# A filter MLP layer by four 64-row tiles, its decay factor moved into the weights, and a transform that begins with the filter

## The chip, the cores and the metric

The kernel runs on one core of a Trainium2 chip. Its time is the device time of one execution in microseconds (us), taken over several runs. TensorE (PE) multiplies matrices, VectorE (DVE), ScalarE (ACT) and GpSimd (POOL) work element by element, and SyncE (SP) issues most of the DMA transfers. PEld is the part of TensorE that loads the stationary operand of a matmul.

## The reference

```
h_mlp  = relu(pos_emb @ w1) @ w2          # 12480 x 64, 64 x 64, 64 x 128
h_filt = h_mlp * exp(-0.01 * pos)         # the window, pos = 0 .. 12479
u      = x * v                            # 12480 x 128
y      = causal convolution of u with h_filt along the sequence, by FFT
a      = x * y
g1 = a @ w_in;  b = (g1 * clip(g1 + 3, 0, 6) / 6) @ w_out        # 128 -> 2048 -> 128
g2 = b @ w_in2; out = elu(g2) @ w_out2                           # 128 -> 2048 -> 128
```

In float32 the window is exactly zero from position 10398 on, so only the first 10398 rows of the filter matter.

## The kernel before, in words

The sequence is folded into 98 blocks of 128 positions (`H1 = 98`, `N2 = 128`); inside a block, position 64+i and position 63-i are paired, for i from 0 to 63 (`HN = 64`). So each i is a column of 98 pairs. The convolution is a transform over the block index (the *first step*, line 324), one over the position inside a block (lines 378, 387, 397), a product (411, 416), and the way back (424, 504). Two MLPs of 2048 hidden units follow (lines 624 to 668), and take most of the time. All engines follow one order written out by hand; nothing reorders it. An engine that waits holds up whatever stands behind it.

The change is at the very start:

- SP loads the position embeddings in eight pieces (line 169, tile `qb<-in_posT`; the pieces end at i = 4, 10, 17, 25, 34, 44, 54, 64), then six chunks of x and v (`uv<-in_xc`, `uv<-in_vc`), and between these the small tables `ratio`, `t1`, `rows`, `column`. Eight transfers are in flight: the ninth is issued when the first has landed, and so on.
- `filter_hidden` (lines 274 to 306) works on groups of columns: i = 0..3, 4..7, then eight at a time, then 56..59 and 60..63. One matmul per i (line 278) has the 98 pairs as its stationary operand, with the 64 features of one position in the upper 64 rows and those of its partner in the lower 64, and a block-diagonal `w1` of 128 columns as the moving one. `relu` (line 286) is done by ACT for the second half, i by i, with the decay ratio of the two partners as its scale. `folds` (line 299) has DVE take the relu of the first half and add and subtract the second; the sums and differences are the *filter pieces'* input `Rf`.
- `signal` (lines 262 to 271) multiplies a chunk of x and v (4 channels) and makes sums and differences. Chunks 0 and 1 are done by POOL, the others by DVE.
- The first step has 48 units of eight matmuls (`first`, line 320): 32 take a signal chunk (`first_u`, kind 0 in `order`), 16 take 4 features of the filter (`first_r`, kind 1). Each ends in one ACT copy (line 327). `first_r` reads all 64 columns of `Rf`, so no such unit can begin before the last fold.

Of the kernel before, what the change touches and what calls it, by code (L numbers as in the profile page):

```python
# [41 lines left out]
NU = KF // 2  # L42
LAG, DELAY = 5, 13
EX = 8
HIDDEN = [(0, 4), (4, 4), *((i, 8) for i in range(8, HN - 8, 8)), (HN - 8, 4), (HN - 4, 4)]
WARM = 6
LEAST, MOST = (float(np.uint32(z).view(np.float32)) for z in (0x38000000, 0x47EFFFFF))

# [11 lines left out]
def tables():  # L60
    n1, k1, k2 = np.arange(H1), np.arange(NK), np.arange(N2)
    i, m, a = np.arange(HN), np.arange(NM), np.arange(H1) - 2 * SHIFT - 1
    w = 2 * np.pi * (np.outer(n1 - SHIFT, k1) % N1) / N1
    c, s = np.cos(w), np.sin(w)

    t1 = np.stack([np.stack([c, -s], axis=2), np.stack([-s, -c], axis=2)], axis=1)
    k = k1[:, None] + N1 * k2
    w = np.pi * (((2 * i + 1)[:, None, None] * k) % (2 * L)) / L
    gm = np.concatenate([np.cos(w), np.sin(w)], axis=0)

    w = 2 * np.pi * (np.outer(k2, m) % N2) / N2
# [12 lines left out]
    rows = t1 * np.exp(-0.01 * N2 * n1)[:, None, None, None]
    column = np.tile(np.exp(-0.01 * (HN + i)), 2)[:, None]
    ratio = np.tile(np.repeat(RATIO, 2), (H1, 1))
    return [np.ascontiguousarray(z, dtype=np.float32) for z in (t1, gm, cs, ti, rows, column, ratio)]


def folded(z):  # L90

    z = np.pad(z, ((0, SP - S), (0, 0))).reshape(H1, N2, -1)
    return np.stack([z[:, HN:], z[:, HN - 1::-1]], axis=1).transpose(0, 3, 1, 2)


@with_exitstack
def tile_kernel(ctx, tc, xc, vc, xT, posT, w1_d, w2_d, moe_w, t1_d, gm_d, cs_d, ti_d, rows_d, column_d, ratio_d, outT):
    nc = tc.nc
    w_dram = [nc.dram_tensor(f"w_scratch{i}", (128, FF), F32, kind="Internal").ap() for i in range(4)]

# [34 lines left out]
    qb = big.tile([128, 2 * QW], F32, name="qb")  # L135
# [22 lines left out]
    assert MB + MW <= RF and RF + D + MW <= 2 * QW - AW - RW  # L158

    pos_t = qb[:, :HP]  # L160
    Rf = qb[:H1, RW:RW + RF].rearrange("p (g s i t) -> p s i g t", s=2, i=HN, t=2)
    Rp = qb[:H1, RW:RW + RF].rearrange("p (g s x) -> p s g x", s=2, x=2 * HN)
    w1s = qb[:, HP:HP + 2 * FO]
    ratio = qb[:H1, HP + 2 * FO:HP + 2 * FO + N2]
    GI = 4
    nc.scalar.dma_start(w1s, w1_d)
    edges = [0, 4, 10, 17, 25, 34, 44, 54, 64]
    for a, b in zip(edges, edges[1:]):
        nc.sync.dma_start(pos_t[:, a * H1:b * H1], posT[:, a * H1:b * H1])
    tab = const.tile([128, 8 * NK], F32, name="tab")  # L170
    t1, rows = (tab[:H1, i * 4 * NK:(i + 1) * 4 * NK].rearrange("p (f k) -> p f k", f=2) for i in range(2))
    qss = [z[:NK, :4 * N2].rearrange("p (d n) -> p d n", n=N2) for z in (tab, au[:, AW:], au[:, S:])]
    thirds = [0]
    column = const.tile([128, 1], F32, name="column")
    cs = const.tile([128, 2 * N2], F32, name="cs")
# [77 lines left out]
    NR = FO // DC  # L253
# [17 lines left out]
        return ut  # L271


    def filter_hidden(i0, n):
        pr = bank("pr", [128, 2, 2, FO // 2, GI, 2])
        t = au[:H1, i0 * FO:(i0 + n) * FO].rearrange("p (b g j t) -> p b g j t", g=FO // 2, j=GI, t=2)
        for j in range(n):
            nc.tensor.matmul(  # L278
                pr[:H1, j // GI, :, :, j % GI], lhsT=pos_t[:, (i0 + j) * H1:(i0 + j + 1) * H1],
                rhs=w1s.rearrange("p (s g t) -> p s g t", s=2, t=2), start=True, stop=True,  # L280
            )
        def relu(b):
            i = i0 + b * GI
            own = GI if i < HN - 2 * GI else 2
            for j in range(own):
                nc.scalar.activation(t[:, b, :, j], pr[:H1, b, 1, :, j], AF.Relu, scale=float(RATIO[i + j]))
            return own

        def folds(b, own):
            i = i0 + b * GI  # L290
            if own < GI:
                nc.vector.scalar_tensor_tensor(
                    t[:, b, :, own:].rearrange("p g j t -> p g (j t)"),
                    pr[:H1, b, 1, :, own:].rearrange("p g j t -> p g (j t)"), 0.0,
                    ratio[:, 2 * (i + own):2 * (i + GI)].unsqueeze(1).to_broadcast([H1, FO // 2, 2 * (GI - own)]),
                    op0=ALU.max, op1=ALU.mult,
                )
            for x, op in enumerate((ALU.add, ALU.subtract)):
                nc.vector.scalar_tensor_tensor(
                    Rp[:, x, :, 2 * i:2 * (i + GI)], pr[:H1, b, 0].rearrange("p g j t -> p g (j t)"), 0.0,  # L300
                    t[:, b].rearrange("p g j t -> p g (j t)"), op0=ALU.max, op1=op,
                )

        owns = [relu(b) for b in range(n // GI)]
        for b, own in enumerate(owns):
            folds(b, own)

    for n in range(DEEP):
        load_signal(n)
        if n == 0:  # L310
            nc.sync.dma_start(ratio, ratio_d)
            nc.sync.dma_start(t1.rearrange("p f k -> p (f k)"), t1_d)
        if n == 1:
            nc.sync.dma_start(rows.rearrange("p f k -> p (f k)"), rows_d)
            nc.sync.dma_start(column, column_d)
# [222 lines left out]
    for m0 in range(0, NM, 2):  # L538
# [208 lines left out]
```

## Time and profile before

| | |
|---|---|
| three runs | 1347.17, 1348.6, 1349.86 us; median 1348.6 |
| profiled execution | span 1346.2 us, from the first to the last instruction; no other time is shown for it |
| busy | PE 99%, PEld 85%, DVE 85%, ACT 74%, POOL 29% of the span |
| filter MLP and its folds | 3.8 to 22 us |
| first step of the transform | 19.4 to 79.1 us |

The share of busy time is an average over the whole program, in which the two MLPs weigh most. The change touches the first 80 us, so it is read from the timeline and the chain of waits there. The timeline prints runs of equal instructions as one row: where it starts, how long it lasts, engine, line, operation, tiles, count, and in brackets the idle time ahead of it with what ended it. One matmul of 32-bit numbers leaves two PE records and two PEld records. In the trace, a row named SPq or ACTq is the issue of a DMA.

### The profile page before, as it was taken

What the parts mean: (1) busy time and instruction counts of PE and PEld (TensorE: products, weight loads), DVE (VectorE), ACT (ScalarE), POOL (GpSimd) and SP (SyncE); (2) the same over time, 40 slices, a digit from 0 to 9 for tenths busy, and PEclk for the clock granted to TensorE, in tenths of its full rate; (3) what the DMA queues carried; (4) which work ended last, traced back from release to release, by engine and by line L of the source; (5) the groups of instructions that cost most, each with busy time, mean ns of one, the idle gap of its engine ahead of it and who ended that gap; (6) DMA issues with size and microseconds to landing.
All of it is one profiled execution on the core that took longest, in us unless ns stands there. A gap on an engine that the chain in (4) does not pass through costs nothing.

```text
span 1346.2 us, 20841 instructions
## 1 busy us (share of the span) xinstructions
PE 1338.7 (99%) x8154; PEld 1148.0 (85%) x8154; DVE 1149.3 (85%) x1230; ACT 992.9 (74%) x1171; POOL 394.4 (29%) x280
## 2 busy tenths in 40 slices
PE   9999999999999999999999999999999999999998
PEld 9999999978888888888888888888888888888898
DVE  6749887799988888888888888888888888888897
ACT  5666633288788877788778878887778877887876
POOL 1027721215322222332222232222233222222223
PEclk9999999999999999999999999999999999999999
DMA  8924319730000000000000000000000000000000
GB/s 268 258 75 142 100 34 293 237 106 1 8 0 9 8 9 9 1 8 9 9 0 9 9 9 1 8 9 9 9 1 8 9 9 1 9 8 9 9 3 17
DMA packets 32490, 58.15 MB, mean 43 GB/s; under 512 B 3879, under 2 KB 12168, under 8 KB 32392
## 3 DMA queue, kind: packets, MB, share of 16 engines
q1 hardware_dynamic: 25192, 48.11, 11.7%
q10 hardware_dynamic: 7200, 8.72, 2.0%
q8 instruction: 64, 1.05, 0.3%
q14 instruction: 34, 0.28, 0.1%
HBM read 46.23 MB, written 10.58 MB: 42 GB/s over the span
## 4 chain that ended last, share of the span: by engine, by line
PE 90%; DVE 5%; issue 2%; ACT 1%; POOL 1%; DMA 1%; SPq 0%; POOLq 0%; DVEq 0%; ACTq 0%
PE h L624 37%; PE o L668 37%; PE pa L324 4%; PE q L424 4%; PE y L504 3%; PE z L397 1%; DVE gs L658 1%; PE pr L278 1%; DVE bp L411 1%; DVE qb L411 1%; PE r L378 1%; PE h L387 1%; DVE cv L210 1%; DVE g L645 1%; DMA qb<-in_posT 0%
## 5 line engine op out<-in xcount | busy, mean ns | idle before, releaser
L668 PE MATMUL o<-gs,w 128*128 128x512 f32 (+1 forms) x2400 | 567.1, 384 | 0.5 <-DVE gs L658 0.3
L668 PEld LDWEIGHTS o<-gs,w 128*128 128x128 f32 x2400 | 445.3, 188 | 88.6 <-DVE gs L658 0.8
L637 POOL TENSOR_SCALAR a<-a 128x1024 f32<-128x1024 f32 (+1 forms) x200 | 294.5, 1472 | 720.0 <-ACT a L636 720.0
L658 DVE TENSOR_TENSOR gs<-g,gs 128x1024 fp32r<-128x1024 f32 (+1 forms) x400 | 482.4, 1206 | 4.5 <-ACT gs L653 3.7
L653 ACT CAST gs<-g 128x1024 fp32r<-128x1024 f32 (+1 forms) x400 | 410.2, 1025 | 54.4 <-DVE g L645 52.8
L645 DVE SCALAR_TENSOR_TENSOR g<-a,h 128x1024 f32<-128x1024 f32 (+1 forms) x200 | 238.6, 1193 | 121.4 <-ACT a L634 121.3
L624 PE MATMUL h<-xs,w 128*128 128x512 f32 (+1 forms) x1200 | 302.1, 387 | 0.4 <-DVE g L645 0.4
L624 PE MATMUL h<-x,w 128*128 128x512 f32 (+1 forms) x1200 | 299.0, 385 | 0.2 <-ACT a L636 0.2
L636 ACT ACTIVATE a<-h 128x1024 f32<-128x1024 f32 (+1 forms) x200 | 201.3, 1006 | 92.7 <-PE h L624 91.5
L624 PEld LDWEIGHTS h<-xs,w 128*128 128x128 f32 x1200 | 223.6, 188 | 48.5 <-DVE g L645 1.4
L624 PEld LDWEIGHTS h<-x,w 128*128 128x128 f32 x1200 | 223.0, 188 | 43.8 <-issue 0.5
L634 ACT ACTIVATE a<-h,bounds 128x1024 f32<-128x1024 f32 (+1 forms) x200 | 218.9, 1095 | 51.8 <-PE h L624 51.6
L647 DVE SCALAR_TENSOR_TENSOR g<-a,h 128x1024 f32<-128x1024 f32 (+1 forms) x200 | 237.2, 1186 | 0.2 <-POOL a L637 0.2
L215 POOL TENSOR_TENSOR cv<-cv 128x256 int32<-128x256 int32 x32 | 23.3, 729 | 96.4 <-DVE cv L212 89.8
L416 POOL TENSOR_TENSOR qb<-qb,bp 128x1024 f32<-128x1024 f32 (+2 forms) x14 | 27.7, 1981 | 71.2 <-DMA qb<-in_gm 70.7
L504 PE MATMUL y<-ti,qb 91*64 91x98 f32 (+1 forms) x1024 | 45.9, 247 | 0.8 <-DVE cv L212 0.5
L504 PEld LDWEIGHTS y<-ti,qb 91*64 91x64 f32 x1024 | 45.4, 138 | 1.3 <-DVE cv L212 0.7
L324 PE MATMUL pa<-tab,cv 98*64 98x182 f32 x512 | 44.5, 318 | 0.0
L324 PEld LDWEIGHTS pa<-tab,cv 98*64 98x64 f32 x512 | 37.6, 137 | 3.9
L198 ACT ACTIVATE cv<-cv 128x256 f32<-128x256 f32 x32 | 14.3, 447 | 35.1 <-DMA cv<-in_mw 16.8
L411 DVE TENSOR_TENSOR qb<-z,qb 128x1024 f32<-128x1024 f32 (+2 forms) x15 | 15.9, 1060 | 17.9 <-ACT qb L390 15.2
L431 DVE TENSOR_TENSOR qb<-q,au 91x512 f32<-91x512 f32 (+2 forms) x44 | 26.4, 650 | 3.8 <-ACT au L429 3.8
(67 smaller groups left out, 832.5 us busy)
## 6 DMA issues: line engine op xcount, KB each, us to landing
uv<-in_xc SPq DMA_DIRECT2D x32, 196.0 KB
out_T<-y SPq DMA_DIRECT2D x23, 256.0 KB
au<-in_xT SPq DMA_DIRECT2D x8, 728.0 KB
qb<-in_gm SPq DMA_DIRECT2D x22, 256.0 KB
ti<-in_ti SPq DMA_DIRECT2D x32, 139.3 KB
cv<-in_mw ACTq DMA_DIRECT2D x17, 256.0 KB
uv<-in_vc SPq DMA_DIRECT2D x22, 196.0 KB
w_scratch<-cv ACTq DMA_DIRECT2D x32, 128.0 KB
```

What stands on the lines that cost most here:

```text
L324: nc.tensor.matmul(pa[f * HN:(f + 1) * HN, j, :2 * NK], lhsT=src(j, f), rhs=table[:, f], start=True, stop=True)
L424: nc.tensor.matmul(q[:NK, r, j], lhsT=Au[hf][:, s0 + j, :, r], rhs=cs[:, r * N2:(r + 1) * N2], start=True, stop=True)
L504: nc.tensor.matmul(y[h * HD:(h + 1) * HD, off:off + w], lhsT=Q[:NK, h, j // 2, :, j % 2], rhs=ti[:, m - m0, r, H1 - w:], start=r == 0, sto ...
L624: nc.tensor.matmul(h[:, j], lhsT=wslice(2 * m - 2, a, 2 * u + j), rhs=x[:, b], start=i == 0, stop=i == 2)
L634: nc.scalar.activation(a, h, AF.Relu, bias=three)
L636: nc.scalar.activation(a, h, AF.Exp)
L637: nc.gpsimd.tensor_scalar(a, a, 1.0, 0.0, op0=ALU.min, op1=ALU.max)
L645: nc.vector.scalar_tensor_tensor(g, a, 6.0, h, op0=ALU.min, op1=ALU.mult)
L647: nc.vector.scalar_tensor_tensor(g, a, -1.0, h, op0=ALU.add, op1=ALU.max)
L653: nc.scalar.copy(t[:, 0], g)
L658: nc.vector.tensor_tensor(out=t[:, 1], in0=g, in1=t[:, 0].bitcast(F32), op=ALU.subtract)
L668: nc.tensor.matmul(o[:, :WID[t]], lhsT=wslice(2 * m - 1, a, 2 * u + j), rhs=gs[:, b, j], start=u == 0 and j == 0 and i == 0, stop=u == NU ...
```

## The change

The second half's decay ratio leaves the activation. It is multiplied into 64 copies of `w1`, one for each i (`w1x`), in partitions 64 to 127: the builds for the first five groups are done by DVE, those for the last four by POOL. Each i is then four matmuls of 64 rows, 64 output partitions and 64 columns: first and second half (r) times two overlapping sets of 64 of the 82 blocks that are left (a: blocks 0 to 63 and 18 to 81; in the table `rows`, the duplicated blocks have zeros). The positions are loaded for 82 blocks instead of 98, in the same eight pieces. `Rf` and the table `rows` now take 128 partitions, the relu and the folds work on 128 partitions and on all columns of a group in one instruction, and the last two groups of four become one of eight. For the groups at i = 24 and i = 48 (`SIDE`), ACT does the relu of both halves and POOL the sum and the difference. The table `ratio` and its load are gone. The first step begins with two filter units instead of two signal units.

```diff
+HR = -(-ZERO // N2)                       # 82
-HP = H1 * HN
+HP = HR * HN
+ROWS = np.concatenate([np.arange(HD), np.arange(HR - HD, HR)])
-HIDDEN = [(0, 4), (4, 4), *((i, 8) for i in range(8, HN - 8, 8)), (HN - 8, 4), (HN - 4, 4)]
+HIDDEN = [(0, 4), (4, 4), *((i, 8) for i in range(8, HN, 8))]
+SIDE = (24, 48)
...
-    w1s = qb[:, HP:HP + 2 * FO]
-    ratio = qb[:H1, HP + 2 * FO:HP + 2 * FO + N2]
+    w1s, ratio = qb[:, HP:HP + FO], qb[HD:, HP + FO:HP + FO + HN]
+    w1x = qb[HD:, HP + FO + HN:HP + FO + HN + HN * FO].rearrange("p (i g) -> p i g", g=FO)
+    nc.scalar.dma_start(qb[:, HP:HP + FO + HN], w1_d)
-        nc.sync.dma_start(pos_t[:, a * H1:b * H1], posT[:, a * H1:b * H1])
+        nc.sync.dma_start(pos_t[:, a * HR:b * HR], posT[:, a * HR:b * HR])
...
+    for k, (i0, n) in enumerate(HIDDEN):
+        (nc.vector if k < 5 else nc.gpsimd).tensor_tensor(
+            out=w1x[:, i0:i0 + n], in0=w1s[HD:].unsqueeze(1).to_broadcast([HD, n, FO]),
+            in1=ratio[:, i0:i0 + n].unsqueeze(2).to_broadcast([HD, n, FO]), op=ALU.mult,
+        )
...
         for j in range(n):
-            nc.tensor.matmul(
-                pr[:H1, j // GI, :, :, j % GI], lhsT=pos_t[:, (i0 + j) * H1:(i0 + j + 1) * H1],
-                rhs=w1s.rearrange("p (s g t) -> p s g t", s=2, t=2), start=True, stop=True,
-            )
+            for a in (0, 1):
+                for r, w in enumerate((w1s[:HD], w1x[:, i0 + j])):
+                    c = (i0 + j) * HR + a * (HR - HD)
+                    nc.tensor.matmul(
+                        pr[a * HD:(a + 1) * HD, r, :, j], lhsT=qb[r * FO:(r + 1) * FO, c:c + HD],
+                        rhs=w.rearrange("p (g t) -> p g t", t=2), start=True, stop=True,
+                    )
+        nc.scalar.activation(t, pr[:, 1, :, :n], AF.Relu)
+        if i0 in SIDE:
+            nc.scalar.activation(t0, pr[:, 0, :, :n], AF.Relu)
+        for x, op in enumerate((ALU.add, ALU.subtract)):
+            to = Rp[:, x, :, 2 * i0:2 * (i0 + n)]
+            a, b = (z.rearrange("p g j t -> p g (j t)") for z in ((t0 if i0 in SIDE else pr[:, 0, :, :n]), t))
+            if i0 in SIDE:
+                nc.gpsimd.tensor_tensor(out=to, in0=a, in1=b, op=op)
+            else:
+                nc.vector.scalar_tensor_tensor(to, a, 0.0, b, op0=ALU.max, op1=op)
...
-    order = [(0, n) for n in range(2)] + [(1, 0), (1, 1)]
-    for c in range(2, NR + 1):
-        order += [(0, 2 * c - 2), (0, 2 * c - 1)] + [(1, c)] * (c < NR)
+    order = [(1, 0), (1, 1)]
+    for c in range(2, NR + 2):
+        order += [(0, 2 * c - 4), (0, 2 * c - 3)] + [(1, c)] * (c < NR)
```

On PE, from the warm-up matmuls to the fifth unit of the first step (`pr` is the filter MLP, `pa` the first step; `cv` holds a signal chunk, `qb` the filter), it stood before:

```order
L131 MATMUL warm<-au 128x128 x6
L278 MATMUL pr<-qb 98x64x2 x64
L324 MATMUL pa<-tab,cv 64x182 x16
L324 MATMUL pa<-tab,qb 64x182 x16
L324 MATMUL pa<-tab,cv 64x182 x16
```

and now:

```order
L134 MATMUL warm<-au 128x128 x6
L293 MATMUL pr<-qb 64x32x2 x256
L323 MATMUL pa<-tab,qb 64x182 x16
L323 MATMUL pa<-tab,cv 64x182 x16
L323 MATMUL pa<-tab,qb 64x182 x8
```

Four small matmuls stand for each one of before, and the two signal units (16 matmuls) have changed places with the two filter units. On POOL, from its first tile operation to its last before the second step (`uv`, `cv` are signal chunks), it stood before:

```order
L267 TENSOR_TENSOR uv<-uv 98x512
L269 TENSOR_TENSOR cv<-uv 98x4x64
L270 TENSOR_TENSOR cv<-uv 98x4x64
L267 TENSOR_TENSOR uv<-uv 98x512
L269 TENSOR_TENSOR cv<-uv 98x4x64
L270 TENSOR_TENSOR cv<-uv 98x4x64
```

and now:

```order
L279 TENSOR_TENSOR qb<-qb 64x512 x4
L304 TENSOR_TENSOR qb<-au 128x32x16 x4
L271 TENSOR_TENSOR uv<-uv 98x512
L273 TENSOR_TENSOR cv<-uv 98x4x64
L274 TENSOR_TENSOR cv<-uv 98x4x64
L271 TENSOR_TENSOR uv<-uv 98x512
L273 TENSOR_TENSOR cv<-uv 98x4x64
L274 TENSOR_TENSOR cv<-uv 98x4x64
```

The two signal chunks that POOL prepares stand behind four builds of scaled weights and behind the folds of two groups. On DVE, from its first operation on the filter to the first signal chunk, it stood before:

```order
L299 SCALAR_TENSOR_TENSOR qb<-pr,au 98x32x8 x28
L292 SCALAR_TENSOR_TENSOR au<-pr,qb 98x32x4
L299 SCALAR_TENSOR_TENSOR qb<-pr,au 98x32x8 x2
L292 SCALAR_TENSOR_TENSOR au<-pr,qb 98x32x4
L299 SCALAR_TENSOR_TENSOR qb<-pr,au 98x32x8 x2
L267 TENSOR_TENSOR uv<-uv 98x512
```

and now:

```order
L279 TENSOR_TENSOR qb<-qb 64x256 x2
L279 TENSOR_TENSOR qb<-qb 64x512 x3
L306 SCALAR_TENSOR_TENSOR qb<-pr,au 128x32x8 x4
L306 SCALAR_TENSOR_TENSOR qb<-pr,au 128x32x16 x10
L271 TENSOR_TENSOR uv<-uv 98x512
```

Five builds of scaled weights stand ahead of the folds, and 32 folds of four columns have become 4 of four and 10 of eight.

## Rows read from the trace of the kernel before

**Rows 1.** Chain that ended last, 0 to 80 us: start us, us, what
```profile
1.65 5.66 DMA qb<-in_posT
...
7.36 12.03 PE pr L278 x108
19.39 59.74 PE pa L324 x728
79.13 3.77 PE r L378 x32
```
**Rows 2.** Groups of instructions by line, 4.5 to 5 us, then 6 to 6.5 us
```profile
L278 PE MATMUL pr<-qb 128*98 128x128 f32 x5 | 1.3, 421 | 0.0
...
L278 PE MATMUL pr<-qb 128*98 128x128 f32 x7 | 0.9, 273 | 0.0
```
**Rows 3.** Timeline of PE in later steps: start us, us, engine, line, operation, count
```profile
24.55 0.32 PE L324 MATMUL pa<-tab,cv 98*64 98x182 f32 x1
24.55 0.32 PE L324 MATMUL pa<-tab,qb 98*64 98x182 f32 x1
...
88.67 2.10 PE L387 MATMUL h<-qb 64*128 64x128 f32 x32
91.09 2.10 PE L397 MATMUL z<-qb 128*128 128x128 f32 x16 [0.31 <-DVE bp L411]
...
233.78 37.23 PE L504 MATMUL y<-ti,qb 91*64 91x98 f32 x872 [0.51 <-DVE cv L212]
```
**Rows 4.** Timeline of SP at the start
```profile
7.33 0.32 SPq L311 DMA_DIRECT2D qb<-in_ratio  x1
...
12.12 0.32 SPq L314 DMA_DIRECT2D tab<-in_rows  x1
13.91 0.36 SPq L315 DMA_DIRECT2D column<-in_column  x1
...
17.12 0.39 SPq L244 DMA_DIRECT2D uv<-in_xc  x1
```
**Rows 5.** Waits on SP, 0 to 20 us: total us, times, longest
```profile
SPq L315 <- DMA qb<-in_posT: 1.5, 1, 1.5
...
SPq L244 <- DMA tab<-in_rows: 0.2, 1, 0.2
```
**Rows 6.** Stretches: PE, PEld, DVE, ACT, POOL busy (instructions), granted clock, DMA share, GB/s
```profile
0.00:10.00 10.00, 8.74 (x56) 8.42 (x57) 1.69 (x7) 3.44 (x17) 0.20 (x4) 1.00 0.79 267
...
70.00:80.00 10.00, 10.00 (x127) 8.89 (x124) 2.12 (x5) 6.57 (x9) 0.00 (x0) 1.00 0.33 113
```
**Rows 7.** Groups by line and form, 0 to 80 us: count, busy us, mean ns, idle before
```profile
L327 ACT ACTIVATE au<-pa 128x728 f32<-128x728 f32 x16 | 12.4, 777 | 6.7 <-PE pa L324 5.4 <-DVE uv L267 1.4
...
L299 DVE SCALAR_TENSOR_TENSOR qb<-pr,au 98x256 f32<-98x256 f32 x32 | 11.5, 417 | 9.2 <-ACT au L286 9.0
L286 ACT ACTIVATE au<-pr 98x64 f32<-98x64 f32 x60 | 7.8, 247 | 9.5 <-PE pr L278 9.5
L267 DVE TENSOR_TENSOR uv<-uv,cv 98x512 f32<-98x512 f32 x10 | 6.8, 684 | 0.0
...
L267 POOL TENSOR_TENSOR uv<-uv 98x512 f32<-98x512 f32 x2 | 2.6, 1278 | 14.6 <-DMA uv<-in_xc 14.6
```
**Rows 8.** Timeline of POOL at the start, then one row of the second step
```profile
15.05 1.27 POOL L267 TENSOR_TENSOR uv<-uv 98x512 f32<-98x512 f32 x1 [14.61 <-DMA uv<-in_xc]
...
17.77 1.29 POOL L267 TENSOR_TENSOR uv<-uv 98x512 f32<-98x512 f32 x1
...
91.25 2.39 POOL L416 TENSOR_TENSOR qb<-qb,bp 128x1024 f32<-128x1024 f32 x1 [70.70 <-DMA qb<-in_gm]
```
**Rows 9.** Timeline of DVE at the end of the folds
```profile
21.37 0.75 DVE L299 SCALAR_TENSOR_TENSOR qb<-pr,au 98x256 f32<-98x256 f32 x2
22.04 0.68 DVE L267 TENSOR_TENSOR uv<-uv 98x512 f32<-98x512 f32 x1
```
**Rows 10.** Timeline of SP at the end of the first step
```profile
63.01 0.32 SPq L245 DMA_DIRECT2D uv<-in_vc  x1
```

More of the change, by code (lines that the diff above doesn't have):

```diff
@@ L83, in tables, with folded, tile_kernel @@
     assert not window[ZERO:].any()
-    rows = t1 * np.exp(-0.01 * N2 * n1)[:, None, None, None]
+    rows = (t1 * np.exp(-0.01 * N2 * n1)[:, None, None, None])[ROWS]
+    rows[HD:2 * HD - (HR - HD)] = 0
     column = np.tile(np.exp(-0.01 * (HN + i)), 2)[:, None]
[L86 to L92, printed above, removed]
+    return [np.ascontiguousarray(z, dtype=np.float32) for z in (t1, gm, cs, ti, rows, column)]
+def folded(z, n=H1):
+    z = np.pad(z, ((0, SP - S), (0, 0))).reshape(H1, N2, -1)[:n]
     return np.stack([z[:, HN:], z[:, HN - 1::-1]], axis=1).transpose(0, 3, 1, 2)
 @with_exitstack
-def tile_kernel(ctx, tc, xc, vc, xT, posT, w1_d, w2_d, moe_w, t1_d, gm_d, cs_d, ti_d, rows_d, column_d, ratio_d, outT):
+def tile_kernel(ctx, tc, xc, vc, xT, posT, w1_d, w2_d, moe_w, t1_d, gm_d, cs_d, ti_d, rows_d, column_d, outT):
     nc = tc.nc
@@ L160, in tile_kernel @@
     pos_t = qb[:, :HP]
-    Rf = qb[:H1, RW:RW + RF].rearrange("p (g s i t) -> p s i g t", s=2, i=HN, t=2)
-    Rp = qb[:H1, RW:RW + RF].rearrange("p (g s x) -> p s g x", s=2, x=2 * HN)
-    w1s = qb[:, HP:HP + 2 * FO]
-    ratio = qb[:H1, HP + 2 * FO:HP + 2 * FO + N2]
-    GI = 4
-    nc.scalar.dma_start(w1s, w1_d)
+    Rf = qb[:, RW:RW + RF].rearrange("p (g s i t) -> p s i g t", s=2, i=HN, t=2)
+    Rp = qb[:, RW:RW + RF].rearrange("p (g s x) -> p s g x", s=2, x=2 * HN)
+    w1s, ratio = qb[:, HP:HP + FO], qb[HD:, HP + FO:HP + FO + HN]
+    w1x = qb[HD:, HP + FO + HN:HP + FO + HN + HN * FO].rearrange("p (i g) -> p i g", g=FO)
+    nc.scalar.dma_start(qb[:, HP:HP + FO + HN], w1_d)
     edges = [0, 4, 10, 17, 25, 34, 44, 54, 64]
     for a, b in zip(edges, edges[1:]):
-        nc.sync.dma_start(pos_t[:, a * H1:b * H1], posT[:, a * H1:b * H1])
+        nc.sync.dma_start(pos_t[:, a * HR:b * HR], posT[:, a * HR:b * HR])
     tab = const.tile([128, 8 * NK], F32, name="tab")
-    t1, rows = (tab[:H1, i * 4 * NK:(i + 1) * 4 * NK].rearrange("p (f k) -> p f k", f=2) for i in range(2))
+    t1, rows = (
+        tab[:n, i * 4 * NK:(i + 1) * 4 * NK].rearrange("p (f k) -> p f k", f=2) for i, n in enumerate((H1, N2))
+    )
     qss = [z[:NK, :4 * N2].rearrange("p (d n) -> p d n", n=N2) for z in (tab, au[:, AW:], au[:, S:])]
@@ L271, in signal @@
         return ut
+    for k, (i0, n) in enumerate(HIDDEN):
[3 more added lines that the diff above has]
+        )
     def filter_hidden(i0, n):
-        pr = bank("pr", [128, 2, 2, FO // 2, GI, 2])
-        t = au[:H1, i0 * FO:(i0 + n) * FO].rearrange("p (b g j t) -> p b g j t", g=FO // 2, j=GI, t=2)
+        pr = bank("pr", [128, 2, FO // 2, 8, 2])
+        t, t0 = (
+            au[:, (i0 + x) * FO:(i0 + x + n) * FO].rearrange("p (g j t) -> p g j t", j=n, t=2) for x in (0, HN)
+        )
@@ L277, in filter_hidden @@
         for j in range(n):
-            nc.tensor.matmul(
-                pr[:H1, j // GI, :, :, j % GI], lhsT=pos_t[:, (i0 + j) * H1:(i0 + j + 1) * H1],
-                rhs=w1s.rearrange("p (s g t) -> p s g t", s=2, t=2), start=True, stop=True,
-            )
[L282 to L302, printed above, removed]
@@ L304, in filter_hidden @@
-        owns = [relu(b) for b in range(n // GI)]
-        for b, own in enumerate(owns):
-            folds(b, own)
+            for a in (0, 1):
[4 more added lines that the diff above has]
+                        rhs=w.rearrange("p (g t) -> p g t", t=2), start=True, stop=True,
+                    )
@@ L310, in tile_kernel @@
         if n == 0:
-            nc.sync.dma_start(ratio, ratio_d)
             nc.sync.dma_start(t1.rearrange("p f k -> p (f k)"), t1_d)
@@ L707 @@
     weights = [inputs["moe_w_in"], w_out[0], inputs["moe2_w_in"], w_out[1]]
-    t1, gm, cs, ti, rows, column, ratio = tables()
-    w1 = np.zeros((2 * FO, 2 * FO), np.float32)
-    for i in range(2):
-        w1[i * FO:(i + 1) * FO, i * FO:(i + 1) * FO] = inputs["w1"]
+    t1, gm, cs, ti, rows, column = tables()
     arrays = {
@@ L715 @@
         "xT": x[ORDER].T,
-        "posT": folded(inputs["pos_emb"]).transpose(2, 1, 3, 0).reshape(2 * FO, HP),
-        "w1": w1,
+        "posT": folded(inputs["pos_emb"], HR).transpose(2, 1, 3, 0).reshape(2 * FO, HP),
+        "w1": np.concatenate([np.tile(inputs["w1"], (2, 1)), np.tile(RATIO.astype(np.float32), (N2, 1))], axis=1),
         "w2": np.tile(inputs["w2"], (2, 1)),
@@ L722 @@
         "ti": ti.reshape(NK, NM, -1),
-        "rows": rows.reshape(H1, -1),
+        "rows": rows.reshape(N2, -1),
         "column": column,
-        "ratio": ratio,
     }
@@ L735 @@
     out = nc.dram_tensor("out_T", (D, S), F32, kind="ExternalOutput").ap()
-    names = ("xc", "vc", "xT", "posT", "w1", "w2", "t1", "gm", "cs", "ti", "rows", "column", "ratio")
+    names = ("xc", "vc", "xT", "posT", "w1", "w2", "t1", "gm", "cs", "ti", "rows", "column")
     g = {k: aps[f"in_{k}"] for k in names}
@@ L740 @@
             tc, g["xc"], g["vc"], g["xT"], g["posT"], g["w1"], g["w2"], [aps[f"in_mw{i}"] for i in range(4)],
-            g["t1"], g["gm"], g["cs"], g["ti"], g["rows"], g["column"], g["ratio"], out,
+            g["t1"], g["gm"], g["cs"], g["ti"], g["rows"], g["column"], out,
         )
```

## Prediction

> **What bounds the kernel now.** The change stays within the first 80 us, so I read the chain of waits of that stretch first. The reader is to see that it is TensorE from the third piece of positions on: 108 records of the filter MLP in 12.03 us, and right behind them the 48 units of the first step, 59.74 us without a gap [rows 1], so 59.74 / 48 = 1.245 us a unit. What the change is worth is therefore how much earlier TensorE enters that gapless stretch, counted at the unit from which nothing holds it up any more. Before, it enters at 19.39 and begins its fourth unit at 19.39 + 3 x 1.245 = 23.12 us.
>
> Then come the transfers. SP's issue of `ratio` at 7.33 stood behind the landing of the third piece, which the chain puts at 7.31 [rows 1, 4]; in the same way the issue of `column` at 13.91 waited for the eighth and last piece [rows 4, 5]. So the positions are in at 13.9, and TensorE is still busy with them until 19.4: its own work binds before. Last come the helpers: POOL does its two signal chunks from 15.05 on, 2.72 us apart [rows 8], and DVE folds until 22 us [rows 9], both under cover of TensorE.
>
> **TensorE's part.** Before, the 108 records are 54 columns i, so 12.03 / 54 = 0.223 us for one matmul of 128 columns. A tile that streams 64 columns takes half of it, 0.111 us. Now each i is four of these, on four quarters of the array. If all four run at once an i costs 0.111 us, if two do 0.223, if none 0.446. The trace shows both halves of this, not the whole. Two matmuls that use different output halves start in the same hundredth of a microsecond (24.55 us), and 32 records of two 64-row halves take 2.10 us, no more than 16 full ones [rows 3]. So rows pair and columns pair; I take 0.111 us, the lower bound, since nothing in the array is shared between the four that is not shared in one of these pairs. The upper bound of the pace is the fourth step: 872 records, each with its weight load, in 37.23 us, 0.0427 us for one [rows 3]. An i is eight such, 0.342 us if they could not follow each other faster.
>
> The Trainium skill speaks against my value here: "TensorE: Matmul & The Clock Gate", section "Wait — 56ns, not 53.3ns?", has matmuls start no closer than about 25 ns however few columns they stream. By it, as an estimate, eight records would make 0.2 us an i and the sum below would come out some 2.4 us slower instead of 1 us faster. The two records that start at the same 24.55 us [rows 3] do not agree with it for different quarters.
>
> **The positions.** 82 of 98 blocks are loaded, 0.837 of the bytes, in as many transfers. If time goes with bytes from the 1.65 us at which the chain sees the first [rows 1], the last piece lands at 1.65 + 0.837 x (13.91 - 1.65) = 11.9 us; if it goes with the number of transfers, at 13.9. I take 12.5, nearer to the bytes. The third piece comes at 6.4 to 7.3, I take 6.9. At 0.111 us an i TensorE keeps up with the pieces, so it is the last one that counts: it brings columns 54 to 63. Columns 54 and 55 end the group at 48 at 12.5 + 2 x 0.11 = 12.7 us, the other eight end the group at 56 at 13.6.
>
> **ACT.** 64 elements take 247 ns and 728 take 777 [rows 7], 0.8 ns for one more, so a relu of 512 takes about 0.6 us. The group at 48 needs two (its folds are POOL's): 12.7 + 1.2 and a tenth for the hand-overs, 14.0. The group at 56 gets its relu by 14.65. The scale that is taken out of ACT is worth nothing here: its 60 small relus, 7.8 us busy, sat 9.5 us waiting for TensorE [rows 7].
>
> **The folds, and what is late next.** DVE does the last two folds of 512 elements: 684 ns for that size on DVE [rows 7] gives 14.65 + 1.3 = 15.95 us. POOL does two for the group at 48: 512 elements take it 1.28 us [rows 7], half of its 1024 takes 1.2 [rows 8]; with 1.3 each they end at 14.0 + 2.6 = 16.6. The filter units need both, so the first begins at 16.7, 2.7 us before the 19.39 of now. But POOL still has both signal chunks to do: behind the folds on its queue stand 2 x 2.72 us, so chunk 0 is ready at 19.35 and chunk 1 at 22.1. TensorE runs its two filter units from 16.7 to 19.2, waits to 19.4, runs a signal unit to 20.65, waits for chunk 1, and begins its fourth unit at 22.15. From there it has what it needs. 22.15 - 23.12 = -1.0 us. The reordering covers only one POOL chunk.
>
> **Costs I set at nothing.** The builds of scaled weights: DVE's five (2 x 0.42, estimated from the slope of its 417 and 684 ns, and 3 x 0.68, 2.9 us) stand ahead of folds that could not start before 6 us anyway; POOL's four (4 x 1.28 = 5.1 us) run from the landing of `w1`, under 4 us, to about 9, while POOL sat idle for 14.6 us before [rows 7]. Its first fold can't begin before about 10.5. Read through broadcast they might take twice as long; then POOL's folds end 2.6 us later and the sum is +1.6 us; less than nothing they can't cost. The table `rows`, now 128 rows, was issued at 12.12 and had landed by 17.12 [rows 4, 5]; with `ratio` gone it is issued one piece earlier and a sixth fewer bytes lie ahead, so about 15.2: in time for 16.7, though not for a start much before that. The signal chunks for later units: the last is issued at 63.01 [rows 10] and the DMA share is 0.33 from 70 us on [rows 6], while TensorE ends at 79.1; 1 us earlier leaves them covered. The second step then moves as a block.
>
> TensorE's clock: its records take 421 ns in the first matmuls and 273 ns from 6 us on [rows 2], though the granted clock reads 1.00, the level of 2.4 GHz, over the whole stretch [rows 6]; so the durations show the slow start, not that column. The first columns are slow after the change too, hidden behind the pieces. But TensorE now idles from 13.6 to 16.7. If it comes back slow, at 421 / 273 = 1.5 to 2 times the duration, the fourth unit begins at 16.7 + 3 x 1.245 x 1.5 to 2 = 22.3 to 24.2 and the sum is -0.8 to +1.1 us. No gap of this kind is in the rows of before.
>
> **The sum.** -1.0 us on the profiled span of 1346.2 gives 1345.2; that span is 2.4 below the median of the runs, and no other time is shown for that execution. On the median of 1348.6 it is 1347.6 us. Bounds of the transfer (11.9 to 13.9), POOL's 1.2 us folds, doubled builds and the clock put this case at 1346.6 to 1350.2 us.
>
> **The rivals.**
> - *Only two quarters at once* (slower). Then TensorE stays the bound: from 6.9 us, 46 columns at 0.223 end the group at 48 at 17.15 instead of 12.7, everything behind it comes 4.4 later, and the sum is +3.4: 1352.0 us. For it: the trace never shows four. Against: each pairing taken by itself is complete. The gain is gone from 0.148 us an i on, and 0.2% is lost from 0.207 on.
> - *Issue pace* (slower). 0.342 us an i ends the group at 48 at 6.9 + 15.7 = 22.6, 9.9 later: +8.9, 1357.5 us. Against: the fourth step's pace is also what two of its matmuls stream, so it need not be a limit.
> - *POOL is not late* (faster). If POOL does folds and chunks in 5.7 us instead of 8.05, DVE's 15.95 decides, four units run back to back from 16.0, the fourth from 19.75: -3.4, 1345.2 us. For it: nothing but that its operands lie elsewhere; its 512 elements took the same in all rows.
> - *Nothing reaches the end.* The earlier start is eaten by a later wait that is set by transfers: 1348.6 us. Against: the DMA share after 70 us.
>
> **Chances.** My case 0.60, two quarters 0.14, issue pace 0.07, POOL not late 0.12, nothing 0.07. What a measurement can tell from no change is about 0.2%, 2.7 us: my case and "nothing" lie within it but for a few hundredths, so faster 0.13, same 0.65, slower 0.22. For 8 in 10 the range goes from 1345.0, just past the faster case, to 1352.6, past the two quarters; the issue pace is left out.
>
> **What would show it.** Right: the filter MLP's matmuls end about 13.6 us, TensorE idles about 3 us, the first unit begins near 16.7 released by POOL's fold, and a second wait, 1.5 us, stands ahead of the fourth unit, for POOL's second chunk; the first step ends near 78.1. Wrong: matmuls of the filter MLP dense until 17 us or later (quarters or pace), or no wait for POOL ahead of the signal units.

## Result and profile after

The changed kernel takes 1357.18 us (median of 5 runs, 1355.98 to 1357.96) against 1347.98 us: a ratio of 1.0064, 95% interval 1.0051 to 1.0076, so 0.6% slower and clear of noise. Forecast was 1347.6, with 1345.0 to 1352.6 as the range. The profiled execution's span is 1355.4 us against 1346.2, its own time 1357.18. The first step ends at 88.70 us instead of 79.13 [rows 1], 9.6 later; the span is 9.2 longer, so what follows takes about as long as before.

The chain of waits of the changed kernel, 0 to 90 us (start us, us, what):

```profile
3.62 5.97 DVE qb L279 x5
...
10.53 0.53 PE pr L293 x18
11.06 1.92 issue
12.98 1.59 PE pr L293 x47
...
23.57 2.50 POOL qb L304 x2
26.07 1.67 POOL uv L271
...
29.47 1.69 POOL uv L271
...
32.93 55.76 PE pa L323 x718
88.70 1.31 PE r L377 x10
```

The end of it is the one forecast: POOL's folds, its two signal chunks, then TensorE without a gap. But the last folds begin at 23.57, not at 14.0. TensorE's own timeline in the filter MLP says why:

```profile
6.74 1.16 PE L293 MATMUL pr<-qb 64*64 64x64 f32 x64 [0.66 <-DVE qb L279]
...
8.20 1.15 PE L293 MATMUL pr<-qb 64*64 64x64 f32 x62 [0.29 <-DVE qb L279]
...
10.53 0.53 PE L293 MATMUL pr<-qb 64*64 64x64 f32 x18 [1.18 <-DVE qb L306]
...
12.98 3.35 PE L293 MATMUL pr<-qb 64*64 64x64 f32 x127 [1.92 <-issue]
...
19.13 4.36 PE L293 MATMUL pr<-qb 64*64 64x64 f32 x175 [2.80 <-issue]
```

When it runs, 64 records (eight columns i) take 1.16 us, and the trace has the starts of two i 0.117 us apart (the 1.16 also hold the tail of the last record): the four quarters do work side by side. But TensorE stands still for 1.92 and 2.80 us with "issue" as the reason: it waits for nothing that the profile shows. Between the two stops lie 127 matmul records, with as many weight loads 254 instructions. The DMA view, 16.5 to 18 us, shows what moves at the second stop, from 16.33 on:

```profile
DMA packets 219, 0.39 MB, mean 258 GB/s; under 512 B 36, under 2 KB 41, under 8 KB 218
...
q8 instruction: 1, 0.02, 5.1%
```

One packet of 0.02 MB (16384 bytes in the trace) belongs to the instruction queue q8; there is none from 12 to 16.5 us. In the trace it is on the way from 16.61 to 17.84 us, and TensorE runs on at 19.13. The packet of the first stop is on the way from 10.27 to 11.55, and TensorE runs on at 12.98. That q8 brings TensorE's instructions is seen from the page of the whole run:

```profile
PE 1338.2 (99%) x8538; PEld 1148.1 (85%) x8538; DVE 1156.9 (85%) x1215; ACT 991.2 (73%) x1122; POOL 406.9 (30%) x288
...
q8 instruction: 67, 1.10, 0.3%
```

Twice 8538 matmul records and loads over 67 packets make 255 a packet, and no other engine on the page has a tenth as many instructions. The Trainium skill describes this ("Runtime: NRT & Kernel Launch", section "Instruction fetch mechanics"): a sequencer refills its instructions in 16 KiB blocks of 256, and the cost is mostly hidden. The block size agrees with the 254 here; "mostly hidden" does not agree with stops of 1.92 and 2.80 us.

The stretches show a second loss (columns as in [rows 6]):

```profile
12.40:15.80 3.40, 2.82 (x104) 2.82 (x108) 1.04 (x2) 1.09 (x2) 0.00 (x0) 0.50 0.94 226
15.80:19.20 3.40, 0.60 (x38) 0.46 (x35) 1.29 (x2) 0.60 (x1) 2.49 (x2) 1.00 0.90 250
19.20:22.60 3.40, 3.40 (x131) 3.40 (x131) 1.27 (x2) 0.79 (x2) 0.00 (x0) 0.50 0.53 173
...
26.00:29.40 3.40, 3.28 (x22) 2.60 (x24) 3.37 (x4) 0.51 (x1) 3.32 (x4) 0.51 0.00 0
29.40:40.00 10.60, 9.85 (x122) 8.54 (x120) 9.53 (x16) 5.85 (x8) 3.40 (x4) 1.00 0.60 185
```

In this profile the granted clock stands at 0.50, 1.2 GHz, for a stretch after each stop. There the starts of two i lie 0.213 us apart in the trace instead of 0.117. The first two filter units run in a third such stretch, after the wait for POOL's folds. The loads of the positions are not late: SP's issue that waits for the last piece stands at 12.86 us.

```profile
12.86 0.34 SPq L248 DMA_DIRECT2D uv<-in_xc  x1
```

Last, the durations (columns as in [rows 7], groups by form, 0 to 90 us):

```profile
L271 POOL TENSOR_TENSOR uv<-uv 98x512 f32<-98x512 f32 x2 | 3.4, 1720 | 0.0
...
L306 DVE SCALAR_TENSOR_TENSOR qb<-pr,au 128x512 f32<-128x512 f32 x10 | 6.3, 684 | 8.2 <-ACT au L297 8.2
L279 POOL TENSOR_TENSOR qb<-qb 64x512 f32<-64x512 f32 x4 | 5.4, 1372 | 3.2 <-DMA qb<-in_w 3.2
L304 POOL TENSOR_TENSOR qb<-au 128x512 f32<-128x512 f32 x4 | 5.0, 1272 | 12.0 <-ACT au L299 12.0
L279 DVE TENSOR_TENSOR qb<-qb 64x512 f32<-64x512 f32 x3 | 4.4, 1533 | 0.0
L297 ACT ACTIVATE au<-pr 128x512 f32<-128x512 f32 x7 | 4.2, 598 | 12.5 <-PE pr L293 12.4
```

DVE's builds take 1533 ns instead of 684, POOL's first product 1720 instead of 1278; POOL's folds and ACT's relus are as priced. DVE's folds keep their 684 ns although some of them run beside POOL's; one of their two inputs, `pr`, is TensorE's output bank, while both inputs of a build or a product are SBUF tiles.

### The profile page after: what moved, and what is told of

It reads as the page before. It is cut to its first block, busy times and chain, and to the rows that moved or that the text cites. A ratio compares the mean times of both kernels' runs of the same rounds, so it can differ in the third digit from the quotient of the medians.

```text
span 1355.4 us, 21542 instructions
## 1 busy us (share of the span) xinstructions
PE 1338.2 (99%) x8538; PEld 1148.1 (85%) x8538; DVE 1156.9 (85%) x1215; ACT 991.2 (73%) x1122; POOL 406.9 (30%) x288
## 4 chain that ended last, share of the span: by engine, by line
PE 88%; DVE 6%; issue 2%; POOL 2%; ACT 1%; DMA 0%; POOLq 0%; DVEq 0%; ACTq 0%
PE h L623 37%; PE o L667 37%; PE q L423 4%; PE pa L323 4%; PE y L503 3%; DVE gs L657 2%; PE z L396 1%; DVE bp L410 1%; DVE qb L410 1%; PE r L377 1%; PE h L386 1%; DVE g L644 1%; DVE cv L214 1%; DVE qb L279 0%; POOL qb L304 0%
## 5 line engine op out<-in xcount | busy, mean ns | idle before, releaser
L503 PE MATMUL y<-ti,qb 91*64 91x97 f32 (+1 forms) x1024 | 45.7, 247 | 0.7 <-issue 0.7
L323 PEld LDWEIGHTS pa<-tab,cv 98*64 98x64 f32 x512 | 41.2, 137 | 3.6 <-POOL cv L273 0.7
L202 ACT ACTIVATE cv<-cv 128x256 f32<-128x256 f32 x32 | 14.3, 446 | 35.4 <-DMA cv<-in_mw 21.5
L323 PE MATMUL pa<-tab,qb 128*64 128x182 f32 x256 | 28.6, 334 | 2.1 <-POOL qb L304 2.1
L410 DVE TENSOR_TENSOR qb<-z,qb 128x1024 f32<-128x1024 f32 (+2 forms) x15 | 15.9, 1063 | 16.8 <-ACT qb L389 14.1
```

Of the source, the lines that this page charges most:

```text
L323: nc.tensor.matmul(pa[f * HN:(f + 1) * HN, j, :2 * NK], lhsT=src(j, f), rhs=table[:, f], start=True, stop=True)
L503: nc.tensor.matmul(y[h * HD:(h + 1) * HD, off:off + w], lhsT=Q[:NK, h, j // 2, :, j % 2], rhs=ti[:, m - m0, r, H1 - w:], start=r == 0, sto ...
```

## Experiments

Times are us; "MLP" is the end of the filter MLP on TensorE, "step" the end of the first step, "0.50" the stretch, reaching into the first step, in which the clock was granted at 0.50. MLP, step and 0.50 come from one profile each; e1 and e7 do the same up to the end of the MLP and differ there by 0.9 us (18.12, 19.05), which shows how far one profile can be trusted.

| kernel | MLP | step | 0.50 | median | ratio to before |
|---|---|---|---|---|---|
| before | 19.39 | 79.13 | none | 1347.98 to 1348.55 | 1 |
| changed | 23.49 | 88.70 | 26.0-29.4 | 1357.18 | 1.0064 (1.0051-1.0076) |
| e1 half the instructions | 18.12 | 87.71 | 22.4-36.0 | 1353.94 | 1.0040 (1.0028-1.0051) |
| e2 builds on DVE | 22.97 | 86.88 | 23.0-29.9 | 1355.18 | 1.0044 (1.0027-1.0061) |
| e3 signal first | 23.15 | 89.64 | 24.0-34.3 | 1359.41 | 1.0083 (1.0066-1.0101) |
| e4 no builds | 22.86 | 87.45 | 17.1-30.7 | 1356.73 | 1.0060 (1.0045-1.0075) |
| e5 halves, no builds | 15.03 | 85.58 | 18.0-35.1 | 1353.15 | 1.0034 (1.0021-1.0047) |
| e7 e1 with fill | 19.05 | 83.82 | none | 1353.99 | 1.0048 (1.0031-1.0064) |
| e8 mixed | 16.72 | 82.22 | 20.6-27.4 | 1351.21 | 1.0026 (1.0016-1.0035) |
| e9 e8 with fill | 16.68 | 80.22 | none | 1349.03 | 1.0019 (1.0000-1.0037) |
| e10 halves, signal first | 16.33 | 78.12 | none | 1346.91 | 0.9999 (0.9985-1.0013) |
| e12 82 blocks alone | 18.48 | 78.26 | none | 1347.43 | 0.9996 (0.9987-1.0005) |

**e1, half the instructions**

```diff
-            for a in (0, 1):
-                for r, w in enumerate((w1s[:HD], w1x[:, i0 + j])):
-                    c = (i0 + j) * HR + a * (HR - HD)
...
+            for r, w in enumerate((w1s[:HD], w1x[:, i0 + j])):
+                c = (i0 + j) * HR
+                nc.tensor.matmul(
+                    pr[:HR, r, :, j], lhsT=qb[r * FO:(r + 1) * FO, c:c + HR],
...
```

`HR` is 82; relus, folds and the table `rows` go from 128 partitions to 82 with it.

> The changed kernel with the two overlapping sets of 64 blocks made one stationary operand of 82 blocks: two matmuls an i instead of four, so half of TensorE's instructions in the filter MLP for the same streaming (two 64-row halves side by side). Builds, POOL's folds, order of units as in the changed kernel. Theory A (TensorE's instructions come in blocks of 256, and it stands idle when it has used one up before the next has come): at most one idle stretch put down to issue inside the filter MLP instead of two of 1.9 and 2.8 us, the fourth unit of the first step begins at 25 to 27 us instead of 32.9, time 1349 to 1351. Theory B (DVE's and POOL's builds and chunks, slower beside each other, are what made it late): builds still 6 us, time within 2 us of 1357. Theory C (four quarters disturb each other): matmuls go faster one by one, no change of the idle stretches.

One stop is left, 1.42 us, on TensorE's timeline:

```profile
10.40 4.32 PE L291 MATMUL pr<-qb 64*82 64x64 f32 x112 [0.95 <-DVE qb L304]
16.14 1.98 PE L291 MATMUL pr<-qb 64*82 64x64 f32 x48 [1.42 <-issue]
```

The MLP ends 5.4 us earlier with DVE's builds still at 5.97 us, as theory A has it. B falls as the whole cause, and C falls: the starts of two i lie 0.147 us apart in the trace, further than with the quarters, and the stops change. The total won only 3.2 us (1357.18 - 1353.94), less than A's 6 to 8: the stretches of this kernel show where the rest went.

```profile
22.40:36.00 13.60, 13.60 (x90) 10.31 (x88) 9.72 (x15) 4.54 (x6) 5.42 (x6) 0.50 0.54 164
36.00:50.00 14.00, 14.00 (x184) 12.86 (x182) 10.27 (x23) 8.95 (x12) 0.00 (x0) 1.00 0.71 215
```

At 0.50 TensorE does 90 records in 13.6 us, at 1.00 it does 184 in 14.0.

**e2, all builds on DVE**

```diff
-        (nc.vector if k < 5 else nc.gpsimd).tensor_tensor(
+        nc.vector.tensor_tensor(
```

> The changed kernel with all nine builds of scaled weights on DVE, none on POOL. Contention theory: DVE's 64x512 builds fall from 1533 to about 690 ns each when POOL does none beside them, all nine end by about 9.3 us (the five ended at 9.6), time -1 to +1 us against the changed kernel, because theory A's idle stretches stay. Rival (the builds are slow because of their broadcast operands): 1.5 us each, nine end at about 15 us, time 2 to 4 us longer. Theory B: with the contention gone the time falls by 4 us or more.

```profile
L279 DVE TENSOR_TENSOR qb<-qb 64x512 f32<-64x512 f32 x7 | 4.3, 699 | 0.0
...
L279 DVE TENSOR_TENSOR qb<-qb 64x256 f32<-64x256 f32 x2 | 0.8, 420 | 2.5 <-DMA qb<-in_w 2.5
```

The contention theory's number: 699 ns by itself, 1533 beside POOL, nine builds done at 8.5. So broadcast costs next to nothing (699 against 684) and the neighbour more than half of the 1533. The Trainium skill has it ("SBUF — State Buffer", section "SBUF: two separate sides"): a DVE operation with two SBUF inputs and a GpSimd operation that reads SBUF exclude each other. The trace agrees that the two hold each other up, but not that they take strict turns: as an estimate, DVE's five builds by themselves (420 and 699 ns) and four of POOL's at the 1278 ns of its product would take 2.9 + 5.1 = 8.0 us in turn, and both engines were through in 5.97. The stops stayed (three, of 2.2 to 2.3 us), and 2.0 us at the median is more than the 1 us expected, though the intervals of the two kernels overlap.

**e3, signal units first** (the three lines of `order` as before the change)

> The changed kernel with the order of units of before (two signal units, then two filter units). If POOL's second signal chunk (ready at 32.9 us) decides, the two signal units end at 34.2, the filter units follow and the fourth unit begins at 35.4 instead of 32.9: 2 to 3 us slower than the changed kernel, 1359.5 to 1360. If the folds decided, no change or up to 1 us faster.

2.2 us slower at the median, the size expected, though the intervals of the two kernels overlap. The chain of the profile is not the expected one:

```profile
22.50 1.23 POOL uv L271
...
23.81 0.74 POOL cv L273
...
24.59 65.05 PE pa L323 x768
89.64 3.77 PE r L377 x32
```

It goes through POOL's first chunk and then through TensorE without a break. In the trace the second chunk was there at 28.6 us, not at 32.9, and the fourth unit began at 33.3, not at 35.4; from 24.0 to 34.3 the clock stood at 0.50. So e3 does not show that POOL's second chunk decides, and what the order by itself costs in the changed kernel stays open.

**e4, no scaled copies**

```diff
-    for k, (i0, n) in enumerate(HIDDEN):
-        (nc.vector if k < 5 else nc.gpsimd).tensor_tensor(
...
-                for r, w in enumerate((w1s[:HD], w1x[:, i0 + j])):
+                for r, w in enumerate((w1s[:HD], w1s[HD:])):
...
-        nc.scalar.activation(t, pr[:, 1, :, :n], AF.Relu)
+        for j in range(n):
+            nc.scalar.activation(t[:, :, j], pr[:, 1, :, j], AF.Relu, scale=float(RATIO[i0 + j]))
```

> The changed kernel without scaled copies: the decay ratio is again the scale of one ACT relu per i, no builds at all; the four 64-row tiles and POOL's folds for two groups stay. Theory A: the same 1024 TensorE instructions of the filter MLP, so idle stretches put down to issue stay (two, 2 to 3 us each); gain against the changed kernel 1 to 3 us, time 1354 to 1356. Theory B: all or nearly all of the loss comes back, time 1348 to 1350.

TensorE's timeline of e4:

```profile
6.50 2.32 PE L287 MATMUL pr<-qb 64*64 64x64 f32 x130 [0.17 <-DMA qb<-in_posT]
11.73 2.09 PE L287 MATMUL pr<-qb 64*64 64x64 f32 x127 [2.91 <-issue]
16.32 3.11 PE L287 MATMUL pr<-qb 64*64 64x64 f32 x127 [2.49 <-issue]
21.30 1.56 PE L287 MATMUL pr<-qb 64*64 64x64 f32 x48 [1.87 <-issue]
```

With no build to wait for, TensorE uses its instructions up sooner and stops three times, again every 127 records; the MLP ends 0.6 us earlier only, less than e1 and e7 differ. Here what the builds cost is hidden behind the supply, not added to it. The rows also price the clock: 127 records take 2.09 us at 1.00, and 3.11 in the row from 16.32 on, in which the clock falls to 0.50 at 17.1. The median is 1356.73, just outside A's 1354 to 1356 and far from B's.

**e13, data transfers held back** (one profile)

```diff
-        load_signal(n)
+        if n < 1:
+            load_signal(n)
...
     for i0, n in HIDDEN:
         filter_hidden(i0, n)
+    for n in range(1, DEEP):
+        load_signal(n, nc.scalar)
```

> The changed kernel with the loads of signal chunks 1 to 5 held back until ACT is through with the filter MLP (issued by ACT): the positions, chunk 0 and the tables are then the only data transfers beside the filter MLP. If instruction transfers are late because they queue among data transfers, the second one starts about 1.2 us after TensorE enters its last block instead of 3.6, the second stop (2.8 us) falls under 1 us and the filter MLP ends at 20.5 to 21.5 instead of 23.5. Rival (the transfer takes as long whatever else moves): no change of the stops. The whole gets no faster, since chunks 1 to 5 come late.

Its timeline of TensorE, and its DMA view from 13.7 to 15.1 us:

```profile
12.72 5.79 PE L293 MATMUL pr<-qb 64*64 64x64 f32 x254 [1.65 <-issue]
19.91 0.93 PE L293 MATMUL pr<-qb 64*64 64x64 f32 x48 [1.40 <-issue]
```

```profile
DMA packets 17, 0.02 MB, mean 15 GB/s; under 512 B 13, under 2 KB 16, under 8 KB 16
...
q8 instruction: 1, 0.02, 5.5%
```

The second instruction packet, on the way at 16.5 us at the earliest in the changed kernel, comes here by 15.1 at the latest, with hardly any data beside it. In the trace it starts 1.05 us after TensorE has entered its block (12.72, 13.77), in the changed kernel 3.63 us after (12.98, 16.61); once on the way it takes 1.2 us in both. The second stop is gone: 254 records in one row. TensorE, faster now, meets a stop of 1.40 us at the next block. The MLP ends at 20.84, in the expected window. So part of a stop goes with the data transfers, and part is there without them. The whole takes 1356.77 us: the late chunks give the gain back, as expected (a filter unit then stands 2.80 us behind a copy of ACT, which has the late loads to issue).

**e5, halves without builds** (the edits of e1 and e4, all folds on DVE), **e8, mixed** (as e5, but the columns below 24 by one block-diagonal matmul each, and the last eight columns as two groups of four)

> Two matmuls an i (82-block stationary operand, two 64-row halves), no scaled copies (ACT relu with a scale per i), all folds on DVE, filter units first: what is left of the change is the row halves, the 82 blocks and the order. Supply theory: 536 TensorE records pairs with the warm-up against about 444 that ran before the first stop in four kernels, so one stop put down to issue, 1.5 to 2.5 us, at the same count (i about 54); the filter MLP ends at 16 to 17, the fourth unit begins at 22.5 to 24, time 1348 to 1351, the upper end if the granted clock falls in the first step. Rival (stops come from the data transfers or the helpers, which are lighter here): no stop, MLP ends at 14, time 1346.

> As e5, but the columns below 24 by one block-diagonal matmul each, as before the change (82 blocks), and the last eight columns as two groups of four: 440 matmul records and as many weight loads, warm-up included, until the filter MLP ends instead of 536 in e5. Supply theory: no stop put down to issue inside the filter MLP; it ends at about 14 (last piece at 12.9), the first filter unit begins at 16 to 16.5, POOL's second chunk is there by 20, the fourth unit begins at about 20.2 against 23.1 before: 1345 to 1346, or up to 1348 where the granted clock falls in the wait ahead of the first step. Rival (stops have nothing to do with the count): a stop as in e5, 1348 to 1351.

e5 had no stop, where the supply theory had one at about 444; its 1353.15 us is longer than either side forecast. e10, below, is e5 with the order and the groups of before. It takes as long for an i, 0.147 us from start to start in the trace, and it does stop there. TensorE's timelines, e5 first, then e10:

```profile
6.90 8.13 PE L285 MATMUL pr<-qb 64*82 64x64 f32 x216 [1.11 <-DMA qb<-in_posT]
17.72 4.88 PE L316 MATMUL pa<-tab,qb 82*64 82x182 f32 x32 [2.68 <-DVE qb L299]
...
6.86 6.37 PE L285 MATMUL pr<-qb 64*82 64x64 f32 x168 [0.37 <-DMA qb<-in_posT]
14.36 1.98 PE L285 MATMUL pr<-qb 64*82 64x64 f32 x48 [1.12 <-issue]
```

So the supply theory in the form "so many instructions, then a stop" is wrong, and the pace alone does not decide either. What counts is whether the next block is there when one is used up. In the trace the packet has landed at 11.48 us in e5 and at 12.87 in e10, and TensorE comes to the end of its block at 13.1 and 13.0. Over all kernels here there are sixteen such stops; they stand after 441 or 445, 699 or 953 loads and matmul records, and TensorE runs on 1.2 to 1.6 us after a packet of q8 has landed. e8 had no stop, as expected, but its MLP ended at 16.7, not 14: its 160 records of halves took 6.08 us, 0.147 us an i, and DVE's folds ran to 19. Both e5 and e8 then met the clock:

```profile
20.60:27.30 6.70, 6.70 (x48) 5.41 (x46) 3.59 (x8) 2.51 (x3) 0.00 (x0) 0.50 0.75 238
27.50:40.00 12.50, 12.50 (x166) 11.65 (x164) 9.18 (x21) 8.04 (x10) 0.00 (x0) 1.00 0.66 199
```

These are e8's stretches; TensorE had waited 2.35 us for the folds just before.

**e7 and e9, TensorE kept busy**

```diff
+    fill = [bank("fill", [128, N2]) for i in range(2)]
+    for i in range(12):
+        nc.tensor.matmul(fill[i % 2], lhsT=zeros, rhs=zeros, start=True, stop=True)
     us = [signal(n) for n in range(LOOK)]
```

> e1 with 12 more 128x128 matmuls of zeros on TensorE between the filter MLP and the first step, 0.22 us each, into a spare bank: nothing else changes. Clock theory: in e1 the clock was granted at 0.5 for 13.7 us of the first step, which cost its 45 units after the fourth 60.5 us instead of 56.0; with TensorE kept busy the clock stays up or falls for less, 2 to 4 us faster than e1, 1350 to 1352. Rival (the clock falls because of the stops earlier, or the loss was the helpers'): no change against e1, 1353.5 to 1354.5.

> e8 with the same 12 matmuls of zeros between filter MLP and first step. If the clock fell in e8: 1 to 3 us faster than e8. If it did not: no change, both about 1345.5, against 1348 before.

In the profiles the clock stands at 1.00 from the first unit on, and the first step ends 3.9 us earlier than in e1 and 2.0 earlier than in e8. The median agrees for e9 (2.2 us less than e8, but the intervals overlap) and not for e7 (no less than e1). The granted clock differs from run to run: of e7's five runs the one with a mean of 1.000 took 1351.33 us, and the three with 0.997 took 1353.99 to 1356.48. So the idle wait ahead of the first step does cost clock in the profiles; how much of it a run pays is not settled by e7.

**e11, slower use** (one profile)

```diff
+            nc.tensor.matmul(pr[:, 0, :, n - 1], lhsT=zeros, rhs=zeros[:, :HD].rearrange("p (g t) -> p g t", t=2), start=True, stop=True)
             for a in (0, 1):
```

> The changed kernel with one matmul of zeros (128 rows, 64 columns) ahead of each i, into a bank that the last column of the group writes over: the four quarters stay, TensorE has 20 records' worth of instructions an i instead of 16, but uses about 55 of them in a us instead of 110. Supply theory: a block of 254 then lasts about 4.6 us against 6 for its replacement, so the stops put down to issue fall from 1.9 and 2.8 us to 1.5 or less each. Rival (the quarters themselves make TensorE stop): stops as in the changed kernel or more.

Inconclusive for what it was made for. TensorE took 1.04 us an i, so that no supply could be late:

```profile
22.33 0.69 PE L290 MATMUL pr<-au 128*128 128x64 f32 x2
22.95 0.49 PE L294 MATMUL pr<-qb 64*64 64x64 f32 x8
23.37 0.69 PE L290 MATMUL pr<-au 128*128 128x64 f32 x2
```

No stop put down to issue was left, which the supply theory asks for, but at a clock of 0.50 and a seventh of the instructions in a microsecond (20 in 1.04 us against 16 in 0.117).

**e10 and e12, what may be left of the change** (e5 with the order and the groups of before; the kernel before with 82 blocks alone)

> The 82 blocks and two 64-row halves of e5 (two matmuls an i, no scaled copies, folds on DVE), with the order of before (two signal units first) and its groups of columns. Row halves let the filter MLP end at 15 instead of 19.4; POOL's chunks are there at 16.6 and 19.3, so the signal units run at 16.7 and 19.3 while DVE ends its folds near 18, and the fourth unit begins at 21.8 against 23.1 before. If the granted clock stays at 1.0 in these two short waits: 1 to 1.5 us faster than before, 1347. If it falls: 1350 to 1352, slower than before.

> The kernel before with 82 blocks of positions instead of 98 and nothing else of the change. TensorE is the bound of the filter MLP from the third piece on, and its 128 columns an i stay: only the start moves, from 7.3 to about 6.3, so 0.5 to 1 us faster, 1347.5. A rival that counts bytes (the loads bind) expects 2 us.

Their first steps end 1.0 and 0.9 us earlier than before (table), e10 with the clock at 1.00 throughout its profile, though with the stop of 1.12 us shown above. Neither is told apart from the kernel before by its times: of e10's eleven runs eight took 1345.78 to 1347.52 us, and three, with a mean clock of 0.994 to 0.995, 1350.85 to 1353.12. Nothing here beats the kernel before measurably. Against e5 the order and the groups of before gave back 6.2 us (1353.15 - 1346.91), the most of all steps here: e5's TensorE stands 2.68 us ahead of its first filter unit and then has the clock at 0.50 for 17 us, while e10's signal units fill that wait.

## Why the prediction was wrong

- *Transfers.* Right: the issue that waits for the last piece stands at 12.86 us (12.5 was taken), the one for the third at 6.29 (6.9).
- *TensorE's part.* The step that failed. "If all four run at once an i costs 0.111 us" came true for the pace: while TensorE runs at 1.00 an i costs 0.117, so neither "two quarters" nor the estimate of 0.2 us came. But "TensorE keeps up with the pieces" took the instructions as given. Four matmuls an i use up 254 instructions in 2.1 us (e4's 127 records at 1.00), and the next block came later than that: two stops, 4.7 us, and the clock at 0.50 behind them stood in its place. e1 (half the instructions: MLP 5.4 us earlier) and e13 (less in the way of the blocks: 2.7 us) show it. The rival "issue pace" gave 1357.5, nearly the measured time, by a steady 0.342 us an i that does not exist: its number is right by luck, its mechanism is not.
- *Builds.* "2.9 us" on DVE was 5.97, since POOL's builds ran beside them and I priced each engine alone. The first folds came at 9.6, not at 6, and TensorE waited until 10.53 for the output bank that they free, with the fifth piece there since 8.1.
- *POOL.* Folds as priced (2.50 against 2.6). Its two chunks took 6.86 us (26.07 to 32.93) instead of 5.44. DVE's chunks, held up with everything else, now ran at the same time, and before they never met; that this is the reason is argued from e2's builds, not tested apart.
- *Clock.* Seen as a risk of -0.8 to +1.1 us from one idle stretch ahead of the first unit. The changed kernel's profile has three stretches at 0.50 and other kernels one of up to 17 us. Two of the three lie in the filter MLP, behind the stops, where the prediction had no stop; the third, in the two filter units, is hidden, because the signal units wait for POOL even so.
- *Sum.* POOL's last folds begin 9.6 us late (23.57 against 14.0). The rows give 4.7 of it for the two stops. The rest are estimates: 2.5 for the 26 columns i up to the group at 48 that ran at 0.213 us instead of 0.117; 1.4 for the builds, since from 10.53 on the 32 columns of the groups at 24 to 48 would have ended at 14.1 even at 0.111 us, instead of 12.7; 0.2 for 0.117 instead of 0.111. Some 0.8 us is not accounted for. With 1.4 for POOL's chunks, and folds 0.1 shorter than priced, the fourth unit has all it needs 10.8 late (32.93 against 22.15), and the step ends 9.6 later than before. The parts do not add up one by one when removed: e4 took the builds away and the supply filled the gap.
- *Order.* Right in kind: a second wait for POOL stands ahead of and within the fourth unit, 0.41 and 0.34 us in the trace where 1.5 was forecast. That the order itself would gain is not borne out: filter units first cost e5 6.2 us against e10, with other groups of columns as the only other difference, and in the changed kernel e3 leaves it open.

## What to carry to other kernels

Many small matmuls side by side need their instructions as fast as they run: count the instructions in a microsecond, and look for "issue" stops of TensorE that come every 254 loads and matmul records, above all while the DMA queues are full. Halving the instructions by a wider stationary operand won 3.2 us. Going back to the signal units first, and to the groups of before, won another 6.2 once the MLP was short: TensorE's waits around the first units fell from 2.68 us (e5) to 0.59 at most (e10), and in the profile the clock stayed at 1.00. Price element-wise work of DVE and POOL together where both inputs of both come from SBUF. And before work that feeds TensorE is put on an idle but slower engine, look at what already stands on that engine's queue: here POOL's chunks waited behind its folds (read from the chain, not tested apart).

## What the runs showed of the hardware

- TensorE ran on 1.2 to 1.6 us after an instruction packet of 16 KB had landed, at all sixteen stops. With the data transfers out of the way the second packet started 1.05 us after TensorE had entered its block instead of 3.63 (e13, one profile).
- A build of 64x512 on DVE costs 699 ns alone and 1533 ns beside POOL's; POOL's 98x512 product cost 1278 alone and 1720 beside DVE's. DVE's folds, with one input from TensorE's bank, kept 684 ns beside POOL's folds.
- Alternating one 128-row matmul with four 64-row ones cost 1.04 us for ten records of little streaming at a clock of 0.50 (e11), against 0.213 for the eight without.
- Four quarters took 0.117 us an i at 1.00, row halves of 82 columns 0.147, and the one block-diagonal matmul of before 0.218, all from start to start in the traces.
